# Attention's subtraction of q's maximum on GpSimd, and routing in five groups that cross the pairs

## The chip, the cores and the metric

The kernel runs on one core of a Trainium2 chip. The metric is the device time of one execution in microseconds, the median of several runs. The core has four compute engines that run side by side, each working through its own instructions in the order in which they were issued: TensorE (PE; its weight loads are shown as PEld), VectorE (DVE), ScalarE (ACT) and GpSimd (POOL). SyncE (SP), ACT and POOL issue DMA transfers. In the trace, SPq, ACTq, POOLq stand for what those engines' sequencers do.

## The reference

Three layers follow one another, all in float32. First linear attention over 8 batches and 8 heads of 576 tokens with 64 dimensions, then a mixture of 8 experts of which each token uses one, then a dense layer with a leaky activation:

```python
q_s = exp(q - max(q, -1));  q_s /= sum(q_s, -1) + 1e-9        # per token and head
k_s = exp(k - max(k, tokens));  k_s /= sum(k_s, tokens) + 1e-9
x = q_s @ (k_s^T @ v)                                          # [4608, 512]
logits = x @ w_gate + modality_bias[modality_id];  e = argmax(logits)
out[token] = prob(e) * (relu(x @ w1[e]) @ w2[e])
h = out @ w_in;  y = maximum(0.01 * h, h) @ w_out
```

## The kernel before

Attention with its routing is the first stage, up to about 193 us of the span; the experts, the hidden layer and the last product follow. Only the first stage is touched.

Batches are taken in four pairs. A pair is nine chunks of 128 tokens, so there are 36 chunks, counted through here from 0 to 35. For each pair `phase_k` works on k: `kmax` (DVE: a maximum over the tokens, L140, and two subtractions, L143), `kexp` (PE transposes, ACT exponentials), `kv` (PE products with v, L164), `krec` and `kvn` (normalise), `kvT` and `kg` (the gate's weights are multiplied in). `phase_q` takes the maximum of q over each head, for three chunks at once (`qmax`, L218), and subtracts it in place (`qsub`, L222), both on DVE. `phase_x` works chunk by chunk: `trans` transposes q on PE and exponentiates on ACT, `xmm` multiplies by k's result on PE and copies the denominators and the gate's logits to the tiles `ri` and `lr` on ACT, and `evac` takes the reciprocal of `ri` (L258) and scales the result out of PSUM (L260) on DVE, from where SP stores it to `xd`.

`phase_r` routes a group of chunks: some twenty small DVE instructions (`r0`, L296, to `r16`, L360), one exponential on ACT (`rx`) and two tiny PE products (`rm`) give each token a row in the table `region`. Then `scat` writes token and gate weight to that row by one indirect DMA for each chunk, issued from GpSimd (L363). `paced` puts a copy of one element of a chunk's `ri` ahead of a scatter on GpSimd (L375), so that the scatter waits until that chunk's reciprocal has been taken.

The order of all this is written out by hand. Every step has a key in chunk lengths (a pair starts at nine times its number; `evac` of chunk c has the key c + 1), the steps are sorted by key, and each engine gets its instructions in that order. The keys order the work; nothing waits for a clock. PSUM holds two chunks' results (`ps_x`), two transposed tiles (`ps_t`) and two of k's (`ps_k`).

Before, pair 0 is routed in one group with its nine scatters paced one chunk apart; pairs 1 to 3 in groups of three chunks, each group's scatters issued together 3.5 chunk lengths after its last chunk; ten groups in all. Behind the last scatter, the experts' first table entry is read from `region` (L546), the tokens' rows are gathered (L553), transposed (L564) and multiplied (L572). Meanwhile DVE works out the slot tables (L431 to L476). In the later hidden layer GpSimd adds tiles of 512 elements (L841, L842, L845) while DVE applies the leak (L814, both inputs in SBUF) and adds out of PSUM (L847).

Of the kernel before, what the change touches and what calls it, by code (L numbers as in the profile page):

```python
# [9 lines left out]
F32 = mybir.dt.float32  # L10
# [3 lines left out]
AF = mybir.ActivationFunctionType  # L14
ALU = mybir.AluOpType
# [4 lines left out]
B, H, S, D = 8, 8, 576, 64  # L20
NT, DM = B * S, H * D
NE, F1, F2 = 8, 1024, 2048
NPAIR = B // 2
NC = 9
# [67 lines left out]
def bc(ap, axis, n):  # L92
    a = ap.unsqueeze(axis)
    shape = list(a.shape)
    shape[axis] = n
    return a.broadcast_to(shape)


def attention(ctx, tc, cst, a, region, xd):

    nc = tc.nc
    ident, onesf, trib, onesb, biasT, tokid = cst["id"], cst["one"], cst["trib"], cst["oneb"], cst["biasT"], cst["tok"]
    kp = ctx.enter_context(tc.tile_pool(name="kp", bufs=2))
    sp = ctx.enter_context(tc.tile_pool(name="sp", bufs=2))
    one = ctx.enter_context(tc.tile_pool(name="one", bufs=1))
# [4 lines left out]
    eps = one.tile([128, 1], F32, name="eps")  # L110
    nc.vector.memset(eps, 1e-9)
    kvx = []
    for i in range(4):
        t = one.tile([128, 4, 146], F32, name=f"kvx{i}")
# [2 lines left out]
        nc.gpsimd.memset(t[64:128, :, 145:146], 1.0)  # L117
        kvx.append(t)
    tacc = cst["tacc"]
    kt, vt, qt, st_b = {}, {}, {}, {}  # L120

    def load_kv(i, hp):
        if hp == 0:
# [86 lines left out]
    def phase_q(i):  # L210
        s = {}

        def heads(n):
            return qt[i].rearrange("p c (h d) -> p (c h) d", d=D)[:, 24 * n:24 * n + 24]

        def qmax(n):
            qm = s[n] = sp.tile([128, 24], F32, tag="qm", name="qm")
            nc.vector.tensor_reduce(out=qm, in_=heads(n), axis=AX.X, op=ALU.max)  # L218

        def qsub(n):  # L220
            v = heads(n)
            nc.vector.tensor_tensor(out=v, in0=v, in1=bc(s[n][:, :], 2, D), op=ALU.subtract)  # L222

        tm, ts = ((0.2, 3.2, 9.5), (1.2, 4.2, 11.5)) if i == 0 else ((4.6, 7.5, 11.5), (5.5, 9.5, 13.5))
        return [(t, qmax, n) for n, t in enumerate(tm)] + [(t, qsub, n) for n, t in enumerate(ts)]

    def phase_x(i):
        s = {}

        def trans(c):  # L230
            tp = ps_t.tile([128, 4, 128], F32, tag="t", name="tq")
            for hp in range(4):
                nc.tensor.transpose(out=tp[:, hp], in_=qt[i][:, c, 128 * hp:128 * hp + 128], identity=ident)
            eq = s["eq", c] = sp.tile([128, 4, 128], F32, tag="eq", name="eq", bufs=3)
            nc.scalar.activation(out=eq, in_=tp, func=AF.Exp)

        def xmm(c):
            if c == 0:
                st_b[i] = (sp.tile([128, NC, 4, 16], F32, tag="lr", name="lr"), sp.tile([128, NC, 4, 2], F32, tag="ri", name="ri"))
            lr, ri = st_b[i]  # L240
            eq = s["eq", c]
            xp = s["xp", c] = ps_x.tile([128, 4, 256], F32, tag="x", name="xp")
            if c < 8:
                kx = kvx[(2 * i + c // 4) % 4]
                for hp in range(4):
                    nc.tensor.matmul(xp[:, hp, 0:146], lhsT=eq[:, hp], rhs=kx[:, hp], start=True, stop=True)
            else:
                for j in range(2):
                    kx = kvx[(2 * i + j) % 4]
                    for hp in range(4):  # L250
                        nc.tensor.matmul(xp[64 * j:64 * j + 64, hp, 0:146], lhsT=eq[:, hp, 64 * j:64 * j + 64],
                                         rhs=kx[:, hp], start=True, stop=True)
            nc.scalar.activation(out=ri[:, c], in_=xp[:, :, 144:146], func=AF.Identity, bias=eps[:, 0:1])
            nc.scalar.copy(out=lr[:, c], in_=xp[:, :, 128:144])

        def evac(c):
            ri = st_b[i][1]
            nc.vector.reciprocal(out=ri[:, c], in_=ri[:, c])  # L258
            xr = sp.tile([128, DM], F32, tag="xr", name="xr", bufs=4)
            nc.vector.tensor_tensor(out=xr.rearrange("p (q j d) -> p q j d", q=4, j=2),  # L260
                                    in0=s["xp", c][:, :, 0:128].rearrange("p q (j d) -> p q j d", j=2),
                                    in1=bc(ri[:, c], 3, D), op=ALU.mult)
            if c < 8:
                r0 = (2 * i + c // 4) * S + 128 * (c % 4)
                nc.sync.dma_start(out=xd[r0:r0 + 128], in_=xr)
            else:
                for j in range(2):
                    r0 = (2 * i + j) * S + 512
                    nc.sync.dma_start(out=xd[r0:r0 + 64], in_=xr[64 * j:64 * j + 64])

        l = []
        for c in range(NC):
            l += [(c - 0.9, trans, c), (c + 0.3, xmm, c), (c + 1.0, evac, c)]
        return l

    def phase_r(i, c0, c1):

        n = c1 - c0
        cs = slice(c0, c1)
        t, rp = {}, {}  # L280

        def r0():
            lr, ri = st_b[i]
            t["lp"] = sp.tile([128, NC, 8, NE], F32, tag="lp", name="lp", bufs=1)[:, 0:n]
            for x in ("lg", "ex", "w"):
                t[x] = sp.tile([128, NC, NE], F32, tag=x, name=x)[:, 0:n]
            for x in ("mx", "gs"):
                t[x] = sp.tile([128, NC], F32, tag=x, name=x)[:, 0:n]
            for x in ("oh", "st"):
                t[x + "f"] = sp.tile([128, 80], F32, tag=x, name=x)[:, 0:NE * (n + 1)]  # L290
                t[x] = t[x + "f"].rearrange("p (e c) -> p e c", e=NE)
            t["tot"] = sp.tile([128, NE], F32, tag="tot", name="tot")
            t["tb"] = sp.tile([128, 2, NE], BF16, tag="tb", name="tb")
            t["ix"] = sp.tile([128, NC], I32, tag="ix", name="ix", bufs=3)
            t["tg"] = sp.tile([128, NC, 2], F32, tag="tg", name="tg", bufs=3)
            nc.vector.tensor_tensor(out=t["lp"].rearrange("p c (q j) e -> p (c q) j e", q=4),  # L296
                                    in0=lr[:, cs].rearrange("p c q (j e) -> p (c q) j e", j=2),
                                    in1=bc(ri[:, cs].rearrange("p c q j -> p (c q) j"), 3, NE), op=ALU.mult)
            nc.scalar.copy(out=t["tg"][:, 0:n, 0], in_=tokid[:, NC * i + c0:NC * i + c1])

        def r1():
            nc.vector.tensor_reduce(out=t["lg"], in_=t["lp"].rearrange("p c h e -> p c e h"), axis=AX.X, op=ALU.add)

        def r2():
            nc.vector.tensor_tensor(out=t["lg"], in0=t["lg"], in1=biasT[:, NC * i + c0:NC * i + c1], op=ALU.add)

        def r3():
            nc.vector.tensor_reduce(out=t["mx"], in_=t["lg"], axis=AX.X, op=ALU.max)
# [62 lines left out]

    pace = one.tile([1, 1], F32, name="pace")

    def paced(i, c, scat, n):
        nc.gpsimd.tensor_copy(out=pace, in_=st_b[i][1][0:1, c, 0, 0:1])  # L375
        scat(n)

    steps = []
# [1 line left out]
    def add(t0, l):  # L380
        for x in l:
            steps.append((t0 + x[0], len(steps)) + tuple(x[1:]))

    for i in range(NPAIR):
        add(NC * (i - 1), phase_k(i) + phase_q(i))
        add(NC * i, phase_x(i))
        if i < 2:
            t0 = -100 + 10 * i
            add(t0, [(t, load_kv, i, hp) for hp, t in enumerate((0, 1, 3, 4))] + [(t, load_q, i, n) for n, t in enumerate((2, 5, 6))])
        else:  # L390
            t0 = NC * (i - 2)
            add(t0, [(0.5 * hp, load_kv, i, hp) for hp in range(4)] + [(7.9, load_q, i, n) for n in range(3)])

    def route(t0, i, c0, c1, times, ts):

        fs, scats = phase_r(i, c0, c1)
        t = 0
        for n, (name, f) in enumerate(fs.items()):
            t = times.get(name, t)
            add(t0 + t, [(0.001 * n, f)])  # L400
        for n, (f, c) in enumerate(scats):
            if isinstance(ts, tuple):
                add(t0 + ts[0] + n, [(0.0, paced, i + 1 + int(ts[0] + n - 1) // NC, int(ts[0] + n - 1) % NC, f, c)])
            else:
                add(t0 + ts, [(0.001 * n, f, c)])

    for i in range(1):
        route(NC * (i + 1), i, 0, NC, dict(r0=1.15, r1=2.5, r2=3.5, rx=4.4, r5=4.5, r8=5.6, rm=6.55, r10=6.6, r12=7.6, r13=7.61, r16=8.5), (9.05,))
    group = dict(r0=0.2, r2=0.6, rx=1.45, r5=1.15, rm=2.25, r10=2.1, r12=2.6)
    for i in range(1, NPAIR):  # L410
        for g in range(3):
            if (i, g) < (NPAIR - 1, 2):
                route(NC * i + 3 * g + 3, i, 3 * g, 3 * g + 3, group, 3.5)
    route(NC * NPAIR, NPAIR - 1, 6, NC, dict(r0=0.2), 0.5)
    add(1.0, [(0.1, cst["prep"])])
    for x in sorted(steps, key=lambda x: x[:2]):
        x[2](*x[3:])
# [573 lines left out]
def build(ctx: ExitStack, tc, a, out, dbg=None):  # L991
# [13 lines left out]
    with tc.manual_schedule():  # L1005
# [37 lines left out]
        with actx:  # L1043
            z = actx.enter_context(tc.tile_pool(name="zp", bufs=1)).tile([128, (NE * NT + SLOT) // 64], F32, name="z")
            nc.vector.memset(z, 0.0)
            nc.scalar.dma_start(out=region.rearrange("(p r) c -> p (r c)", p=128), in_=z)
            attention(actx, tc, cst, a, region, xd)
# [66 lines left out]
```

## Time and profile before

| | |
|---|---|
| median of 3 runs | 1421.89 us (1420.99 to 1422.07) |
| the profiled execution, its own time | 1421.04 us |
| its span in the trace | 1419.2 us |
| busy over the span | PE 1311.5 us (92%), DVE 1047.6 (74%), ACT 586.8 (41%), POOL 289.0 (20%) |
| mean granted TensorE clock | 0.972 of full speed |

The busy shares are means over all stages; the first stage, one seventh of the span, is read by itself below. In the trace's rows an engine's busy time counts instructions only, not the time in which its sequencer waits; the bracket at the end of a row is the engine's idle time before it and what ended that time.

### The profile page before, as it was taken

What the parts mean: (1) busy time and instruction counts of PE and PEld (TensorE: products, weight loads), DVE (VectorE), ACT (ScalarE), POOL (GpSimd) and SP (SyncE); (2) the same over time, 40 slices, a digit from 0 to 9 for tenths busy, and PEclk for the clock granted to TensorE, in tenths of its full rate; (3) what the DMA queues carried; (4) which work ended last, traced back from release to release, by engine and by line L of the source; (5) the groups of instructions that cost most, each with busy time, mean ns of one, the idle gap of its engine ahead of it and who ended that gap; (6) DMA issues with size and microseconds to landing.
All of it is one profiled execution on the core that took longest, in us unless ns stands there. A gap on an engine that the chain in (4) does not pass through costs nothing.

```text
span 1419.2 us, 23583 instructions
## 1 busy us (share of the span) xinstructions
PE 1311.5 (92%) x9189; PEld 1224.6 (86%) x9189; DVE 1047.6 (74%) x1504; ACT 586.8 (41%) x924; POOL 289.0 (20%) x249
## 2 busy tenths in 40 slices
PE   5987719999999999998999999999989999999998
PEld 5876717778777877787999999999989999999998
DVE  4889846867786777746677777787767777877785
ACT  3545415455545554556223323232333333333342
POOL 0004431101110011001334343434321101111111
PEclk9999869999999999999999999999999999999999
DMA  9763246778777878686933332333595343434330
GB/s 371 284 246 127 76 156 232 259 240 279 259 255 247 275 254 263 194 311 195 407 146 134 135 119 104 136 148 120 233 417 205 122 134 123 149 120 134 119 119 30
DMA packets 146970, 279.57 MB, mean 197 GB/s; under 512 B 18208, under 2 KB 70432, under 8 KB 145952
## 3 DMA queue, kind: packets, MB, share of 16 engines
q1 hardware_dynamic: 122064, 208.46, 43.1%
q10 hardware_dynamic: 17232, 48.48, 8.7%
q0 software_dynamic: 7552, 21.02, 4.1%
q8 instruction: 75, 1.23, 0.4%
q14 instruction: 47, 0.39, 0.1%
HBM read 181.59 MB, written 96.32 MB: 196 GB/s over the span
## 4 chain that ended last, share of the span: by engine, by line
issue 26%; DVE 8%; PE 7%; POOL 6%; DMA 3%; ACT 1%; POOLq 0%; SPq 0%; DVEq 0%
PE hp L801 7%; POOL out L982 3%; DMA wi<-wid 2%; POOL s L841 2%; DVE ht L814 1%; DMA hd<-ht 1%; DVE ht L850 1%; DVE ht L847 1%; DVE s L838 1%; DVE x L482 1%; DVE ht L834 1%; DVE s L836 1%; POOL s L842 1%; DVE xl L482 0%; ACT ht L843 0%
## 5 line engine op out<-in xcount | busy, mean ns | idle before, releaser
L801 PE MATMUL hp<-xh,wi 128*128 128x256 f32 x1152 | 212.8, 281 | 4.2 <-DVE ht L850 2.3
L960 PE MATMUL yp<-wi,x 128*128 128x256 f32 x1152 | 191.2, 283 | 0.6 <-DVE x L482 0.6
L801 PEld LDWEIGHTS hp<-xh,wi 128*128 128x128 f32 x1152 | 179.4, 188 | 6.8 <-DVE ht L850 3.7
L960 PE MATMUL yp<-wi,wi 128*128 128x256 f32 x1200 | 178.2, 283 | 0.3 <-DVE wi L482 0.3
L801 PE MATMUL hp<-x,wi 128*128 128x256 f32 x1296 | 164.5, 286 | 9.2 <-ACTq L708 6.4
L801 PEld LDWEIGHTS hp<-x,wi 128*128 128x128 f32 x1296 | 161.0, 195 | 9.6 <-ACTq L708 6.6
L960 PEld LDWEIGHTS yp<-wi,wi 128*128 128x128 f32 x1200 | 163.5, 192 | 0.5 <-DVE wi L482 0.5
L960 PEld LDWEIGHTS yp<-wi,x 128*128 128x128 f32 x1152 | 161.5, 192 | 0.8 <-DVE x L482 0.8
L801 PE MATMUL hp<-xl,wi 128*128 128x256 f32 x576 | 160.7, 279 | 0.0
L553 POOL DMA_INDIRECT xg<-xd,idi x44 | 55.6, 1264 | 398.6 <-DVE hl L575 331.6
L572 PE MATMUL hp<-xh,w1h 128*128 128x512 f32 (+1 forms) x320 | 122.9, 384 | 11.8 <-DVE hl L575 11.2
L583 PE MATMUL yp<-hh,w2h 128*128 128x512 f32 (+1 forms) x320 | 122.9, 384 | 0.0
L572 PE MATMUL hp<-xl,w1h 128*128 128x512 f32 (+1 forms) x320 | 121.6, 380 | 0.0
L572 PE MATMUL hp<-xh,w1l 128*128 128x512 f32 (+1 forms) x320 | 121.6, 380 | 0.0
L583 PE MATMUL yp<-hl,w2h 128*128 128x512 f32 (+1 forms) x320 | 121.5, 380 | 0.0
L583 PE MATMUL yp<-hh,w2l 128*128 128x512 f32 (+1 forms) x320 | 121.4, 379 | 0.0
L982 POOL DMA_INDIRECT out<-yo,idx x36 | 47.4, 1317 | 315.9 <-DVE idx L976 294.3
L482 DVE TENSOR_TENSOR w1l<-st,w1h 128x1024 fp32r<-128x1024 f32 x44 | 53.8, 1227 | 76.5 <-ACT w1h L481 74.1
L801 PEld LDWEIGHTS hp<-xl,wi 128*128 128x128 f32 x576 | 108.0, 187 | 0.0
L814 DVE SCALAR_TENSOR_TENSOR ht<-ht 128x1024 f32<-128x1024 f32 x72 | 104.9, 1457 | 2.5
L841 POOL TENSOR_TENSOR s<-s,s 128x512 f32<-128x512 f32 x36 | 48.7, 1352 | 209.3 <-DVE s L838 163.8
L843 ACT ACTIVATE ht<-s 128x512 f32<-128x512 f32 x36 | 22.8, 633 | 151.5 <-POOL s L842 147.0
(202 smaller groups left out, 2583.5 us busy)
## 6 DMA issues: line engine op xcount, KB each, us to landing
st<-in_w SPq DMA_DIRECT2D x89, 512.0 KB, 6.5
hd<-ht ACTq DMA_DIRECT2D x72, 512.0 KB, 2.9
xt<-hd SPq DMA_DIRECT2D x18, 1024.0 KB, 5.3
hr<-hd SPq DMA_DIRECT2D x18, 1024.0 KB, 5.2
wi<-wid SPq DMA_DIRECT2D x28, 512.0 KB, 10.3
wi<-wod SPq DMA_DIRECT2D x6, 2048.0 KB, 13.1
v<-in_v SPq DMA_DIRECT2D x16, 650.0 KB, 9.7
k<-in_k SPq DMA_DIRECT2D x16, 576.0 KB, 9.4
```

The lines of the kernel that those rows point to most:

```text
L482: nc.vector.tensor_tensor(out=lo, in0=src, in1=hi.bitcast(F32), op=ALU.subtract)
L553: nc.gpsimd.indirect_dma_start(out=xg[:, t], out_offset=None, in_=xd, in_offset=bass.IndirectOffsetOnAxis(ap=idi[:, t:t + 1], axis=0), bou ...
L572: nc.tensor.matmul(hp[:, rows], lhsT=w[:, k, 128 * f:128 * f + 128], rhs=x[:, k, rows], start=(n == 0), stop=(n == 11))
L583: nc.tensor.matmul(yp[:, rows], lhsT=w[:, f, 128 * d:128 * d + 128], rhs=h[:, f, rows], start=(n == 0), stop=(n == 23))
L801: self.nc.tensor.matmul(bank[:, g], lhsT=w[:, h, k, 128 * g:128 * g + 128], rhs=x[:, k], start=(n == 0), stop=(n == 5))
L814: V.scalar_tensor_tensor(out=c, in0=c, scalar=0.01, in1=c, op0=ALU.mult, op1=ALU.max)
L834: V.tensor_tensor(out=h[:, 0, 0], in0=bank, in1=s[1], op=ALU.add)
L836: V.tensor_tensor(out=s[6], in0=bank, in1=s[1], op=ALU.add)
L841: G.tensor_tensor(out=s[6], in0=s[6], in1=s[5], op=ALU.add)
L843: nc.scalar.activation(out=h[:, 1, 1], in_=s[5], func=AF.Relu)
L960: nc.tensor.matmul(bank, lhsT=x[:, k], rhs=w[i][:, h, k], start=(c == 0), stop=(c == 23))
L982: ins = nc.gpsimd.indirect_dma_start(out=out, out_offset=bass.IndirectOffsetOnAxis(ap=idi[s % 2][:, t:t + 1], axis=0), in_=y[:, t], in_off ...
```

## The change

`qsub` is issued on GpSimd instead of DVE, with the same operands, and the keys of `qmax` and `qsub` are moved, some by up to 1.5 chunk lengths earlier. `lr` and `ri` become one tile each for all 36 chunks. Routing works on any run of chunks: 0 to 8, 9 to 17, 18 to 26, 27 to 32 and 33 to 35, five groups, the third of them with a time table of its own (`mid`). The scatters of the first three groups are paced, 1.0, 0.7 and 0.5 chunk lengths apart; those of the fourth (six) and fifth (three) stand at the end, at the same key.

```diff
@@ phase_q
-            nc.vector.tensor_tensor(out=v, in0=v, in1=bc(s[n][:, :], 2, D), op=ALU.subtract)
-        tm, ts = ((0.2, 3.2, 9.5), (1.2, 4.2, 11.5)) if i == 0 else ((4.6, 7.5, 11.5), (5.5, 9.5, 13.5))
+            nc.gpsimd.tensor_tensor(out=v, in0=v, in1=bc(s[n][:, :], 2, D), op=ALU.subtract)
+        tm, ts = ((0.2, 3.2, 9.5), (1.2, 4.2, 10.5)) if i == 0 else ((4.6, 7.5, 11.0), (5.2, 8.5, 12.0))
@@ attention, phase_x, phase_r: one lr and one ri, indexed by NC * i + c
+    lr = one.tile([128, NPAIR * NC, 4, 16], F32, name="lr")
+    ri = one.tile([128, NPAIR * NC, 4, 2], F32, name="ri")
@@ pacing and routing
-    def paced(i, c, scat, n):
-        nc.gpsimd.tensor_copy(out=pace, in_=st_b[i][1][0:1, c, 0, 0:1])
+    def paced(c, scat, n):
+        nc.gpsimd.tensor_copy(out=pace, in_=ri[0:1, c, 0, 0:1])
         scat(n)
-            if isinstance(ts, tuple):
-                add(t0 + ts[0] + n, [(0.0, paced, i + 1 + int(ts[0] + n - 1) // NC, int(ts[0] + n - 1) % NC, f, c)])
+            if rate:
+                at = c1 + ts + rate * n
+                add(at, [(0.0, paced, min(int(at) - 1, NPAIR * NC - 1), f, c)])
             else:
-                add(t0 + ts, [(0.001 * n, f, c)])
+                add(c1 + ts, [(0.001 * n, f, c)])
-    for i in range(1):
-        route(NC * (i + 1), i, 0, NC, dict(r0=1.15, r1=2.5, r2=3.5, rx=4.4, r5=4.5, r8=5.6, rm=6.55, r10=6.6, r12=7.6, r13=7.61, r16=8.5), (9.05,))
-    group = dict(r0=0.2, r2=0.6, rx=1.45, r5=1.15, rm=2.25, r10=2.1, r12=2.6)
-    for i in range(1, NPAIR):
-        for g in range(3):
-            if (i, g) < (NPAIR - 1, 2):
-                route(NC * i + 3 * g + 3, i, 3 * g, 3 * g + 3, group, 3.5)
-    route(NC * NPAIR, NPAIR - 1, 6, NC, dict(r0=0.2), 0.5)
+    slow = dict(r0=1.15, r1=2.5, r2=3.5, rx=4.4, r5=4.5, r8=5.6, rm=6.55, r10=6.6, r12=7.6, r13=7.61, r16=8.5)
+    mid = dict(r0=0.2, r1=0.9, r2=1.2, rx=2.1, r5=2.15, r8=2.6, rm=3.3, r10=3.4, r12=4.1, r16=4.6)
+    fast = dict(r0=0.2, r2=0.6, rx=1.45, r5=1.15, rm=2.25, r10=2.1, r12=2.6)
+    route(0, 9, slow, 9.05, 1.0)
+    route(9, 18, slow, 9.05, 0.7)
+    route(18, 27, mid, 5.05, 0.5)
+    route(27, 33, fast, 3.5)
+    route(33, 36, dict(r0=0.2), 0.5)
```

## Rows read from the trace of the kernel before

**Rows 1.** Windows: busy us of each engine (instructions), granted clock, DMA share, GB/s.
```profile
45.50:77.70 32.20, 30.02 (x258) 28.80 (x257) 27.19 (x49) 19.84 (x62) 0.00 (x0) 1.00 0.72 262
77.70:120.30 42.60, 34.37 (x272) 32.58 (x271) 39.44 (x109) 21.42 (x72) 6.24 (x6) 0.92 0.58 218
120.30:151.20 30.90, 23.75 (x188) 22.45 (x186) 26.94 (x80) 15.49 (x51) 16.80 (x23) 0.89 0.17 61
151.20:192.60 41.40, 19.97 (x144) 18.11 (x141) 34.80 (x143) 10.84 (x41) 17.64 (x17) 0.82 0.22 71
```
After the window and its length the order is PE, PEld, DVE, ACT, POOL.

**Rows 2.** Timeline of DVE: start, us, engine, line, operation [idle before].
```profile
145.75 0.16 DVE L170 TENSOR_SCALAR rk<-kvp 128x2 f32<-128x2 f32 x1 [0.47 <-PE kvp L164]
...
147.48 0.20 DVE L258 RECIPROCAL ri<-ri 128x8 f32<-128x8 f32 x1 [0.87 <-ACT ri L253]
```

**Rows 3.** Timeline around one subtraction on DVE.
```profile
167.88 1.75 DVE L222 TENSOR_TENSOR q<-q,qm 128x1536 f32<-128x1536 f32 x1
169.55 0.20 DVE L258 RECIPROCAL ri<-ri 128x8 f32<-128x8 f32 x1
169.70 0.72 PEld L233 LDWEIGHTS tq<-cf,q 128*128 128x128 f32 x4 [4.07 <-issue]
```

**Rows 4.** Timeline from the last scatters to the experts' first matmul.
```profile
185.91 1.02 POOL L363 DMA_INDIRECT region<-tg,ix  x1 [3.93 <-issue]
...
191.65 0.99 POOL L363 DMA_INDIRECT region<-tg,ix  x1 [0.30 <-issue]
...
194.00 0.36 SPq L546 DMA_DIRECT2D idt<-region  x1
...
212.99 0.78 PE L572 MATMUL hp<-xh,w1h 128*128 128x512 f32 x1
```

**Rows 5.** DVE by line and shape, 0 to 200 us: busy us, mean ns, idle before.
```profile
L222 DVE TENSOR_TENSOR q<-q,qm 128x1536 f32<-128x1536 f32 x12 | 20.9, 1745 | 0.0
...
L302 DVE TENSOR_REDUCE lg<-lp 128x24 f32<-128x192 f32 x9 | 4.5, 503 | 0.3
L296 DVE TENSOR_TENSOR lp<-lr,ri 128x192 f32<-128x192 f32 x9 | 3.2, 353 | 0.0
...
L302 DVE TENSOR_REDUCE lg<-lp 128x72 f32<-128x576 f32 x1 | 1.2, 1198 | 0.0
...
L296 DVE TENSOR_TENSOR lp<-lr,ri 128x576 f32<-128x576 f32 x1 | 0.8, 751 | 0.0
```

**Rows 6.** Timeline of DVE, first and last of the last group's 20 instructions.
```profile
181.16 0.35 DVE L296 TENSOR_TENSOR lp<-lr,ri 128x192 f32<-128x192 f32 x1
...
184.97 0.17 DVE L360 CAST ix<-mx 128x3 int32<-128x3 f32 x1
```

**Rows 7.** Timeline of DVE and POOL in the hidden layer.
```profile
683.04 1.29 POOL L845 TENSOR_TENSOR ht<-ht,s 128x512 f32<-128x512 f32 x1 [1.41 <-ACT s L844]
683.35 1.53 DVE L814 SCALAR_TENSOR_TENSOR ht<-ht 128x512 f32<-128x512 f32 x1
...
804.99 0.69 DVE L814 SCALAR_TENSOR_TENSOR ht<-ht 128x512 f32<-128x512 f32 x1
...
809.14 0.69 DVE L847 TENSOR_TENSOR ht<-hp,s 128x512 f32<-128x512 f32 x1 [1.47 <-POOL s L841]
809.19 1.30 POOL L842 TENSOR_TENSOR s<-s,s 128x512 f32<-128x512 f32 x1
```

**Rows 8.** POOL by line and shape, 0 to 200 us.
```profile
L115 POOL MEMSET kvx<- 128x584 f32 x4 | 2.4, 588 | 0.5 <-POOLq L1106 0.3
```

**Rows 9.** Timeline of POOL: scatters and paced scatters of the first group.
```profile
148.44 0.97 POOL L363 DMA_INDIRECT region<-tg,ix  x1 [0.30 <-issue]
...
149.73 0.98 POOL L363 DMA_INDIRECT region<-tg,ix  x1 [0.16 <-issue]
...
151.52 0.18 POOL L375 COPY pace<-ri 1x1 f32<-1x1 f32 x1 [0.80 <-DVE ri L258]
152.26 0.98 POOL L363 DMA_INDIRECT region<-tg,ix  x1 [0.57 <-issue]
```

## What I predict, before seeing the result

> **What bounds the kernel now.** I read the page's forty slices first, to see which stretch holds everything the change touches: attention with its routing, up to about 193 us of the span. Then I cut that stretch with the windows view at the reciprocals of chunks 0, 9, 18 and 25 and at the end of the last scatter [rows 1], because the order written out by hand is in chunk numbers. The reader should compare DVE with PE in each row. In the first window (chunks 0 to 9) PE is busy 30.0 of 32.2 us at full clock, DVE only 27.2. In the second DVE is busy 39.4 of 42.6, PE 34.4 at a mean clock of 0.92; counted by instructions (272 against 258 in the first row) PE would need 31.7. In the third DVE is busy 26.9 of 30.9; what is left is mostly two waits for a chunk, 0.5 and 0.9 us [rows 2], and some reading latency. In the fourth DVE is busy 34.8 of 41.4, and the rest is the tail, in which GpSimd issues scatters.
>
> The timeline says the same in small: the DVE subtraction at 167.88 takes 1.75 us, and the transposes of the chunks that it feeds begin at 169.70, when it ends [rows 3]. So pair 0 is bound by PE, pairs 1 and 2 by DVE, pair 3 by DVE and then by the scatters. What comes after cannot start early: the last scatter goes out at 191.65, the expert phase reads the table at 194.00, and its first matmul stands at 212.99 [rows 4]. This chain only moves with the last scatter, so a microsecond won or lost there is one at the end.
>
> **What leaves DVE.** Twelve subtractions at 1.745 us [rows 5]; 1.66 us from start to start, as one overlaps its neighbour a little. Two lie before 45 us, where the loads set the pace and nothing is gained. Of the other ten, three fall in window 1, three in window 2, two in window 3, two in window 4.
> Routing: ten groups become five. A group of three chunks takes 20 DVE instructions, 3.9 us from 181.16 to the end at 185.14 [rows 6]. For nine chunks the reduction grows from 503 to 1198 ns and the product from 353 to 751 [rows 5], so I take 5.0 us, and 4.5 for six. By the keys, window 2 loses groups 9:12 and 12:15 and a third of 15:18 (9.1 us), window 3 exchanges 8.7 us of small groups for most of 9:18 (4.9): 3.8; window 4 exchanges 17.3 for 13.5: 3.8.
> DVE left to do: window 2, 42.6 - 5.0 - 9.1 = 28.5; window 3, 30.9 - 1.3 (the two waits) - 3.3 - 3.8 = 22.5; window 4 up to the last group's end, 33.9 (151.2 to 185.14) - 3.3 - 3.8 = 26.8.
>
> **What GpSimd takes on.** It shows no 1536-element subtraction. Its nearest row is a 128x512 add at 1.29 us [rows 7], three times which is 3.9; from below, its memset of 584 elements at 588 ns [rows 8] would give 1.55. The row of the same operation is nearest: 3.7. From a maximum to the first transpose that needs it the written order leaves at least 3.1 chunk-lengths (for chunks 15, 24 and 33), about 9 us, so a subtraction that starts at once is in time. Four of them stand in GpSimd's queue behind copies that wait for a chunk's reciprocal, and PE's transposes wait behind them in turn; the closest is pair 3's third, behind five scatters: by the sum below it ends some 18.5 us after chunk 25's reciprocal, and chunk 33 is due at about 20. The maxima stay on DVE, half a chunk earlier in places; the single `lr` and `ri` tiles and the new order issue no load or store that was not there.
>
> **What it costs DVE.** The two engines are not independent. DVE's two-input operation on 512 elements takes 0.69 us at 804.99, with no add beside it. At 683.35, begun 0.3 us into a GpSimd add, it takes 1.53 and ends 0.55 us after that add; an operation with one input in PSUM, at 809.14, takes 0.69 beside an add [rows 7]. So a DVE instruction with both inputs in SBUF waits until GpSimd's instruction is over, and an evacuation does not. With the subtraction running for 3.7 us after its maximum, I ask what DVE meets next in the written order. In window 2: third subtraction of pair 1, two evacuations and two reductions, nothing within 3.7 us. First of pair 2: `tacc`'s sum after 1.35 us, so 2.35 lost. Second of pair 2: the scan after 0.3, so 3.4 lost. In window 4: second of pair 3, the product of group 18:27, 3.4 lost; third of pair 3, inside the same group's chain, about 2. In the other places it first meets a subtraction of k's maximum or another one-input operation. No row has one of these beside a GpSimd add: nothing by the evacuation's row, the full rest (1.2 in window 3 at the k subtraction, 2.7 at the denominator) by the two-input row; I take the middle, 1.95 in window 3, and keep both ends.
> The Trainium skill, "SBUF — State Buffer", section "Who interferes with whom", calls this an exclusive lock held for the whole instruction and counts a one-input DVE copy or scalar operation in a two-port mode among those that block. The trace agrees for two inputs (1.53 against 0.69 us) and shows nothing for one; by that rule window 3 would lose 3.9 instead of 1.95.
>
> Window 2 is then 28.5 + 5.75 = 34.25, beside PE's 31.7; window 1 shows that two nearly equal engines lose some time to each other (32.2 for 30.0), so I add 1.5: 35.7, a gain of 6.9. Window 3: 22.5 + 1.95 + 0.6 = 25.0, a gain of 5.9. Window 1 is PE's: a gain of 0.7 at most of the 2.2 that PE does not use. Sum of the gains: 13.5.
>
> **What the scatters cost.** All 36 remain, at 1.0 us each, but they bunch later. From chunk 25 on GpSimd now has, in this order: the ninth scatter of group 0:9, a subtraction, five scatters, a subtraction, thirteen scatters, then nine more (six of 27:33 and three of 33:36, interleaved); before, the window held 16 scatters and no subtraction. A paced scatter that waits costs 2.05 us from the reciprocal (copy 0.18, gap, transfer ended at 153.24); one that is not kept waiting follows at 1.29 (148.44 to 149.73, its copy inside) [rows 9]. I take 1.35 for those eighteen, 1.3 for the last nine (185.91 to 191.65 is 1.43 each, with DVE's table work beside them [rows 4]), 3.85 for a subtraction with its gap, and 1.1 for the wait for chunk 28: 2.05 + 7.7 + 24.3 + 11.7 + 1.1 = 46.9 us. From below 44.6 (1.29 each throughout, no wait), from above 52.4 (1.72 for each paced one, 151.52 to 153.24, a copy that never hides). DVE's own path is 26.8 + 5.4 of waiting + 0.8 (185.14 to 185.91) + 8 scatters behind the last group's first (10.4) = 43.4, shorter: here GpSimd becomes the bound. Before, the stretch took 41.4. Loss: 5.5. The table work on DVE, 7 us behind the last group, is over before the scatters and stays hidden.
>
> Sum: 0.7 + 6.9 + 5.9 - 5.5 = 8.0 us. The profiled execution took 1421.04 us (span 1419.2), so 1413.0; the median of the runs is 0.85 above it: 1413.9, say 1414.
>
> **The rivals.** Differences under 0.2%, 2.8 us, are about what a measurement cannot tell from none.
> *The engines hardly meet* (0.14): what falls beside a subtraction has one input. Then window 2 is PE's at 32.5, window 3 23.0, and the scatters go at their lower bound: 0.7 + 10.1 + 7.9 - 3.2 = 15.5, so 1406.4. For it: only two clear collisions in window 2. Against: the pair of 0.69 and 1.53.
> *One-input operations are held as well* (0.14): window 3 takes 27.0 and gains 3.9, so 1416. In window 1 PE covers the two holds of 1.3 us. That is the rule of the page named above; the trace has no row for or against it.
> *The gain is given back by GpSimd's queue* (0.12): each paced scatter costs its full 1.72, the last window takes 52.4, loses 11.0, and 2.5 us are left: 1419.4, no change that can be told. For it: the waiting copies [rows 9]; against: those that hide.
> *DVE is held for the whole of each subtraction* (0.18): ten holds of 3.7 in place of ten instructions of 1.66. Window 1 becomes 34.8 (2.6 lost), window 2 41.1 (1.5 won), window 3 30.6 (0.3 won), and the last loses 6.5 as its group 18:27 comes late: 7.3 slower, 1429. It decides from a mean hold of about 3 us; I count 1.4. For it: DVE, once stopped, stops the evacuations, and so PE, behind it.
> That nothing changes at all is excluded by the rows: DVE is what the second window waits for, and the order of the scatters differs.
>
> **Numbers.** My forecast has 0.42, its own range 1409 to 1419. Faster: 0.42 + 0.14 + 0.10 of the held one-input case = 0.66; no change 0.12 + 0.04 = 0.16; slower 0.18. The range for 8 in 10 reaches from the first rival to within the last: 1406 to 1425.
>
> **What would show it.** The subtraction as a GpSimd row of 3.4 to 3.9 us; DVE instructions stretched beside it (the scan and `tacc`'s sum above all) and the evacuations not; the stretch from chunk 9's reciprocal to chunk 18's at 34 to 37 us; GpSimd issuing without a pause from chunk 28 to the read of the table; the last scatter some 47 us after chunk 25's reciprocal and near 184 us of the span. Wrong if the subtraction takes over 5 us, if a transpose waits for it, or if the scatters keep up so well that DVE's last group still sets the end.

## The result and the profile after

The changed kernel takes 1409.27 us (median; 1407.18 to 1410.61), the kernel before 1421.44 beside it on the same chip: a ratio of 0.9914, 95% interval 0.9897 to 0.9931, so 12.2 us faster. I had said 1414, in a range of 1406 to 1425. The profiled execution took 1407.18 us, with a span of 1405.4. The helpers have moved by a line or two: the subtraction is L224, an evacuation L259.

First the same four windows as in [rows 1], cut at the reciprocals of the same chunks (start, length, then PE, PEld, DVE, ACT, POOL, granted clock, DMA share, GB/s):

```profile
45.90:76.60 30.70, 29.89 (x258) 28.87 (x257) 22.92 (x47) 19.75 (x62) 8.28 (x3) 1.00 0.75 263
76.60:110.80 34.20, 30.63 (x260) 28.88 (x259) 31.07 (x61) 20.02 (x64) 9.48 (x5) 1.00 0.71 267
110.80:135.20 24.40, 23.31 (x199) 22.03 (x198) 22.19 (x49) 16.10 (x53) 13.72 (x17) 1.00 0.27 88
135.20:180.30 45.10, 19.22 (x133) 16.66 (x132) 35.52 (x114) 10.27 (x37) 37.17 (x49) 0.76 0.22 65
```

The windows gained 1.5, 8.4 and 6.5 us and the last one lost 3.7. PE and DVE are now about level in the second window (30.6 and 31.1 of 34.2), PE is the busier engine of the third, and the granted clock is at the upper level throughout the first three (before: 0.92 and 0.89 in the second and third). In the fourth, POOL is the busiest engine, where it was DVE.

Then GpSimd's timeline, its subtractions from the first of the pair of chunks 18 to 26 on (start, us, operation, idle before):

```profile
92.30 2.76 POOL L224 TENSOR_TENSOR q<-q,qm 128x1536 f32<-128x1536 f32 x1 [7.22 <-DMA xd<-xr]
...
101.88 2.76 POOL L224 TENSOR_TENSOR q<-q,qm 128x1536 f32<-128x1536 f32 x1 [6.81 <-DVE oh L345]
118.87 2.77 POOL L224 TENSOR_TENSOR q<-q,qm 128x1536 f32<-128x1536 f32 x1
128.79 2.77 POOL L224 TENSOR_TENSOR q<-q,qm 128x1536 f32<-128x1536 f32 x1
...
137.28 2.77 POOL L224 TENSOR_TENSOR q<-q,qm 128x1536 f32<-128x1536 f32 x1
...
148.57 2.77 POOL L224 TENSOR_TENSOR q<-q,qm 128x1536 f32<-128x1536 f32 x1
```

(92.30 and 101.88 are the first and second of that pair's three, 118.87 its third; the other three belong to the last pair.) And DVE's timeline, the instructions that fell beside them:

```profile
93.22 1.87 DVE L327 CAST tb<-tacc 128x8 bf16<-128x8 f32 x1
...
101.91 2.91 DVE L349 TENSOR_TENSOR_SCAN st<-cf,oh 128x80 f32<-128x80 f32 x1
...
129.64 1.96 DVE L342 TENSOR_SCALAR gs<-gs 128x9 f32<-128x9 f32 x1
...
137.27 3.40 DVE L294 TENSOR_TENSOR lp<-lr,ri 128x576 f32<-128x576 f32 x1
...
148.67 2.70 DVE L342 TENSOR_SCALAR gs<-gs 128x9 f32<-128x9 f32 x1
```

With no subtraction beside them the same operations take 0.16, 0.33, 0.17, 0.75 and 0.17 us. The reader should lay the two lists over each other: each long DVE instruction ends within 0.7 us of the end of a GpSimd subtraction (148.57 + 2.77 = 151.34; 148.67 + 2.70 = 151.37). I call the time that such an instruction takes beyond its usual one a hold. Three of the five have one input only. An evacuation, a reduction and a reciprocal that begin inside a subtraction are not held; the row that I had read for the evacuation before (809.14 in [rows 7]) began 0.05 us ahead of the GpSimd addition and could not show it, these can:

```profile
82.32 2.76 POOL L224 TENSOR_TENSOR q<-q,qm 128x1536 f32<-128x1536 f32 x1 [12.28 <-DVE qm L220]
82.55 0.69 DVE L259 TENSOR_TENSOR xr<-xp,ri 128x512 f32<-128x512 f32 x1 [0.20 <-DVE ri L257]
...
83.42 1.19 DVE L300 TENSOR_REDUCE lg<-lp 128x72 f32<-128x576 f32 x1
84.54 0.19 DVE L257 RECIPROCAL ri<-ri 128x8 f32<-128x8 f32 x1
...
L259 DVE TENSOR_TENSOR xr<-xp,ri 128x512 f32<-128x512 f32 x36 | 24.9, 692 | 7.7 <-DVE ri L257 2.4 <-ACT ek L162 1.7 <-PE rp L333 0.4
```

The last is a row of the groups by shape (busy us, mean ns, idle before): 692 ns on average over all 36 evacuations. Last, the timeline at the end of the stage, to compare with [rows 4]:

```profile
168.67 0.17 DVE L358 CAST ix<-mx 128x3 int32<-128x3 f32 x1
...
168.86 0.97 POOL L361 DMA_INDIRECT region<-tg,ix  x1 [0.30 <-issue]
...
179.31 0.97 POOL L361 DMA_INDIRECT region<-tg,ix  x1 [0.30 <-issue]
...
181.64 0.37 SPq L546 DMA_DIRECT2D idt<-region  x1
...
200.64 0.78 PE L572 MATMUL hp<-xh,w1h 128*128 128x512 f32 x1
```

DVE is done with its last group at 168.84; nine scatters are still to go out, one every 1.3 us, and the table is read at 181.64 instead of 194.00. The first expert matmul comes 12.35 us earlier, about the 12.2 of the medians.

### The profile page after: what moved, and what is told of

It reads as the page before. It is cut to its first block, busy times and chain, and to the rows that moved or that the text cites. A ratio compares the mean times of both kernels' runs of the same rounds, so it can differ in the third digit from the quotient of the medians.

```text
span 1405.4 us, 23487 instructions
## 1 busy us (share of the span) xinstructions
PE 1306.8 (93%) x9179; PEld 1219.4 (87%) x9179; DVE 1029.1 (73%) x1392; ACT 585.5 (42%) x914; POOL 322.0 (23%) x279
## 4 chain that ended last, share of the span: by engine, by line
issue 26%; DVE 8%; PE 8%; POOL 6%; DMA 3%; ACT 1%; POOLq 0%; SPq 0%; DVEq 0%; ACTq 0%
PE hp L801 8%; POOL out L982 3%; POOL s L841 2%; DMA wi<-wid 2%; DMA hd<-ht 2%; DVE ht L814 1%; DVE ht L847 1%; DVE ht L850 1%; DVE s L838 1%; DVE x L482 1%; DVE ht L834 1%; DVE s L836 1%; POOL s L842 1%; DVE xl L482 0%; ACT ht L843 0%
## 5 line engine op out<-in xcount | busy, mean ns | idle before, releaser
L801 PE MATMUL hp<-x,wi 128*128 128x256 f32 x1296 | 164.2, 286 | 8.0 <-DVEq L708 6.5
L801 PEld LDWEIGHTS hp<-x,wi 128*128 128x128 f32 x1296 | 160.7, 194 | 8.3 <-ACTq L708 6.6
L801 PE MATMUL hp<-xl,wi 128*128 128x256 f32 x576 | 160.7, 279 | 0.0
L572 PE MATMUL hp<-xh,w1h 128*128 128x512 f32 (+1 forms) x320 | 122.9, 384 | 12.7 <-DVE hl L575 11.6
```

What stands on the lines that cost most here:

```text
L572: nc.tensor.matmul(hp[:, rows], lhsT=w[:, k, 128 * f:128 * f + 128], rhs=x[:, k, rows], start=(n == 0), stop=(n == 11))
L801: self.nc.tensor.matmul(bank[:, g], lhsT=w[:, h, k, 128 * g:128 * g + 128], rhs=x[:, k], start=(n == 0), stop=(n == 5))
```

## The experiments

All ratios are against the kernel before; the changed kernel stands at 0.9914. The experiments are numbered in the order in which they ran and told in the order of the argument. Windows are cut as above.

**Experiment 1: the subtractions back on DVE, the merged groups kept.**

```diff
-            nc.gpsimd.tensor_tensor(out=v, in0=v, in1=bc(s[n][:, :], 2, D), op=ALU.subtract)
+            nc.vector.tensor_tensor(out=v, in0=v, in1=bc(s[n][:, :], 2, D), op=ALU.subtract)
```

> The changed kernel with the twelve subtractions back on DVE and everything else (keys, five groups, pacing) as changed. My theory: merging the routing groups paid nearly everything, and the move to GpSimd nearly nothing, because each subtraction that leaves DVE (1.66 us) comes back as holds (1.7 and 2.6 us in the second window, 1.8 in the third). So: window 1 +0.8, window 2 +0.7, window 3 +1.5, last window -2.3 (GpSimd's chain is 5.5 us shorter, then DVE's last group and the eight scatters behind it set the end): about 0.7 us slower than the changed kernel, 1410 (1408 to 1413). Rival, the move is what pays: ten times 1.66 us come back, 1420 or more. Rival, GpSimd's chain alone sets the whole result: 5.5 us faster, 1404.

1415.43 us, 0.9957 (0.9943 to 0.9972): a miss. The merging (with the new keys, the pacing and the single `lr` and `ri` tiles kept, which no run takes apart) is worth 6 us without the move, and the move is worth another 6 on top of it, more than I had left for it. The second window takes 35.9 us (34.2 in the changed kernel), the third 25.6 (24.4), the last 47.8 (45.1). The first takes 32.2 us, as in the kernel before, and 30.7 in experiment 2, which has the move without the merging: the 1.5 us of that window are the move's. The last number is not the subtractions' alone: in this profile ACT stands still near its end (below).

**Experiment 2: the move alone, the ten old groups kept.** The kernel before with `nc.gpsimd` in `qsub` and the new keys of `qmax` and `qsub`.

> The kernel before with the subtractions on GpSimd at their new keys, and the old ten groups and scatters. My theory: the subtractions leave DVE (16.6 us over ten) but DVE is held beside most of them by one-input and two-input operations alike, about 2 us each; window 2 and 3 together win 2 to 4 us, the tail has no bunched scatters, so nothing is lost there: 1418 (1414 to 1421). Rival, the move is what pays: 1410 or less. Rival, holds cost more than the move brings: 1422 or more.

1422.3 us, 1.0003 (0.9992 to 1.0014): a miss too, no change at all, as the rival had it by which holds cost more than the move brings. So 6 from the one part, 0 from the other, 12 from both: the parts don't add up. The trace says why. DVE by line and shape, 76 to 185 us:

```profile
L351 DVE TENSOR_TENSOR_SCAN st<-cf,oh 128x32 f32<-128x32 f32 x8 | 10.4, 1299 | 0.0
...
L344 DVE TENSOR_SCALAR gs<-gs 128x3 f32<-128x3 f32 x8 | 4.6, 569 | 0.3
...
L351 DVE TENSOR_TENSOR_SCAN st<-cf,oh 128x80 f32<-128x80 f32 x1 | 2.9, 2906 | 0.0
```

The scan of a group of three takes 215 ns in the kernel before, 1299 on average here. The timelines of DVE and POOL show single ones:

```profile
128.49 2.89 DVE L351 TENSOR_TENSOR_SCAN st<-cf,oh 128x32 f32<-128x32 f32 x1
128.51 2.77 POOL L222 TENSOR_TENSOR q<-q,qm 128x1536 f32<-128x1536 f32 x1
...
142.51 3.00 DVE L351 TENSOR_TENSOR_SCAN st<-cf,oh 128x32 f32<-128x32 f32 x1
142.66 2.77 POOL L222 TENSOR_TENSOR q<-q,qm 128x1536 f32<-128x1536 f32 x1
```

Six instructions are held in this stretch: four scans (2.9, 2.9, 3.0 and 3.5 us) and two additions to the denominator (1.8 and 1.7). Less what they take anyway (0.33, 0.21 and 0.17), that is 14.5 us, against seven subtractions of 1.66 that left DVE there, 11.6 us. The gain is used up by the holds.

**Experiment 9: the move alone, at other places in DVE's order.** If that is so, the same work at other places must pay. Experiment 2 with, for pairs 1 to 3, each maximum and subtraction put behind the scan of the group before:

```diff
-        ... else ((4.6, 7.5, 11.0), (5.2, 8.5, 12.0))
+        ... else ((5.65, 8.65, 11.65), (5.66, 8.66, 11.66))
```

> The kernel before with the subtractions on GpSimd and its ten groups kept, as in the second experiment, but each maximum and subtraction of q for pairs 1 to 3 stands behind the scan of the group before it (5.65, 8.65, 11.65 chunks instead of 4.6, 7.5, 11.0). If the move alone paid nothing because DVE was held for 2.9, 2.9, 3.0 and 3.5 us at scans that came up while GpSimd subtracted, then no scan takes over 1 us, the holds fall from some 13 us to under 5, and the time is 1414 us (1411 to 1417). The rival: what the move alone lacks is the merging of the groups, wherever the subtractions stand, and the time stays at 1420 to 1424.

1415.38 us, 0.9956 (0.9943 to 0.9969): as expected. The same view as in experiment 2:

```profile
L296 DVE TENSOR_TENSOR lp<-lr,ri 128x192 f32<-128x192 f32 x9 | 10.7, 1192 | 0.0
L351 DVE TENSOR_TENSOR_SCAN st<-cf,oh 128x32 f32<-128x32 f32 x9 | 1.9, 207 | 0.0
L344 DVE TENSOR_SCALAR gs<-gs 128x3 f32<-128x3 f32 x9 | 1.6, 176 | 0.3
```

The scan is back at 207 ns and the addition at 176. What is held now is the product that begins the next group (four of nine, 2.1 to 2.5 us; 1192 ns on average instead of 353), 7.6 us of holds where experiment 2 had 14.5, and three subtractions of k's maximum are held 0.3 to 0.4 us each; that is more than the 5 I had allowed. The time fell by 6.9 us. The second window falls from 43.9 to 40.5 us, the third from 33.7 to 26.8, together more than the 6 to 7 us of holds that are gone; the granted clock rose with them (0.96 and 0.94 for 0.88 and 0.85). Not an instruction was taken out and only places were changed, so what the move is worth hangs on where it stands in DVE's order.

**Experiment 10: no subtraction on any engine.** The changed kernel without the line that issues `qsub` (q is not shifted before the exponential; the maxima are formed).

> The changed kernel without its twelve subtractions on any engine (the maxima are still formed; the shift of q before the exponential is left out). What the subtractions still cost there is then all gone: holds of some 10 us on DVE in the stretch from chunk 9 on, a wait of 1.5 us of TensorE, and 2.8 us of GpSimd's queue each. If they are what my sum said, the stretches from chunk 9 to 18, 18 to 25 and 25 to the last scatter become 32, 23.5 and 40 us, and the time is 1400 us (1397 to 1403). The rival: TensorE bounds the stretches anyway and the scatters the last one, and the time is 1405 to 1409.

1399.32 us, 0.9856 (0.9839 to 0.9873): as expected, with windows of

```profile
76.30:108.84 32.54, 30.55 (x260) 28.95 (x259) 26.80 (x61) 20.08 (x64) 1.31 (x2) 1.00 0.76 284
108.84:131.12 22.28, 21.98 (x190) 21.12 (x188) 20.46 (x49) 15.55 (x50) 8.09 (x14) 1.00 0.24 84
131.12:171.19 40.07, 18.88 (x141) 16.93 (x139) 29.81 (x114) 10.58 (x39) 31.25 (x47) 0.79 0.24 74
```

So twelve subtractions cost some 9 us on GpSimd (the last scatter ends at 171.19 instead of 180.28; the medians are 10 apart, the ratios 8) and 16 on DVE (experiment 1, its standstill of ACT included). Five of the 9 are in the last window, where they stand in GpSimd's queue.

**Experiment 4: smaller holds.** Each subtraction as three of 512 elements.

```diff
-            nc.gpsimd.tensor_tensor(out=v, in0=v, in1=bc(s[n][:, :], 2, D), op=ALU.subtract)
+            for g in range(3):
+                w = slice(8 * g, 8 * g + 8)
+                nc.gpsimd.tensor_tensor(out=v[:, w], in0=v[:, w], in1=bc(s[n][:, w], 2, D), op=ALU.subtract)
```

> The changed kernel with each subtraction cut into three GpSimd instructions of 512 elements. My theory: a hold lasts to the end of the one instruction that is running, so holds fall from 1.7 to 2.7 us to under 1.0 each; window 2 falls from 34.2 to about 32 (PE, busy 30.6 of it, is then the bound), window 3 by 0.5 at most, the last window does not fall, since GpSimd's chain is there the bound and gets some 0.3 us longer for each subtraction: 1407 (1405.5 to 1408.5). Rival, DVE waits until GpSimd's queue is idle: the holds stay as long, 1409 to 1410.

1413.01 us, 0.9941 (0.9929 to 0.9953): a miss. The mechanism works where I looked for it: the scan that took 2.91 us takes 1.19, so DVE waits for the GpSimd instruction under way and gets in before the next, and the second window falls to 33.4 us. But the product behind that scan, at 100.11, is then held by the next third, 0.89 us instead of 0.23: the two holds together are 1.5 us, not 0.86. The last window takes 50.9, 5.8 longer. ACT's timeline there:

```profile
166.82 0.27 ACT L254 ACTIVATE ri<-xp,eps 128x8 f32<-128x8 f32 x1 [8.81 <-remote]
```

It waits for PE's product for chunk 35 and nothing else in the program; that product ended at 159.64 (157.87 and 1.77), 7.2 us before.

**Experiments 3, 5, 6, 11 and 7: GpSimd's queue in the last window.** In experiment 3 the six scatters of chunks 27 to 32 go ahead of the last three:

```diff
-    route(27, 33, fast, 3.5)
+    route(27, 33, fast, 3.4)
```

> The changed kernel with the six scatters of group 27:33 ahead of the last group's three instead of interleaved with them (one key, 3.4 for 3.5). My theory: GpSimd's queue is what ends last, and it has the same nine scatters to issue behind the paced ones, so nothing changes: 1409 within 1.5 us, the last scatter again 45 us after chunk 25's reciprocal. Rival, DVE's last group sets the end (its first scatter waits for DVE and eight follow): now three follow, 5 to 6 us less, 1404.

1410.04 us, 0.9918 (0.9904 to 0.9931): the same, as expected, though in its profile ACT stands still (below) and the last window takes 47.6 us, not 45. In experiment 5 the second group is routed early, with the third's keys:

```diff
-    route(9, 18, slow, 9.05, 0.7)
+    route(9, 18, mid, 5.05, 0.5)
```

> The changed kernel with group 9:18 on the time table of group 18:27 (its scatters start 5.05 chunk lengths after its last chunk, half a chunk apart, instead of 9.05 and 0.7). Nine of the 27 scatters behind chunk 25 then lie before it, and GpSimd's last stretch loses some 12 us of its 45.1. My theory: two chains end together there. DVE's is 33.7 us from chunk 25's reciprocal to the last group's end, 0.8 to its first scatter, and eight scatters of 1.28 behind the same queue: 44.7. So the end moves by half a microsecond only: 1409 (1407 to 1411). Rival, GpSimd's chain alone is the bound: 4 to 8 us less, 1401 to 1405.

1413.06 us, 0.9945 (0.993 to 0.996): a miss. Experiment 6 has both edits:

> The same, and the six scatters of group 27:33 ahead of the last three, which changed nothing by itself. My theory: GpSimd has time for the six while DVE works on the last group, so only three follow it: 33.7 + 0.8 + 3.8 = 38.3; the slot tables on DVE, 7 us behind the last group and 1.9 to the read of the table, then end last, the read comes at 42.5 after chunk 25's reciprocal instead of 46.5: 4 us less than the changed kernel, 1405 (1403 to 1407). Rival, the chain ahead of DVE's last group has grown or ACT stands still there for some other reason: 1408 or more.

1410.73 us, 0.9925 (0.9909 to 0.9942): a miss. PE's timeline of experiment 5 names a wait that the changed kernel has in small (1.50 us, at 151.39):

```profile
149.54 1.12 PE L235 MATMUL tq<-cf,q 128*128 128x128 f32 x4 [6.03 <-POOL q L224]
```

The maximum ended at 136.95 and its subtraction began at 146.71, behind paced scatters in GpSimd's queue; the transposes waited for it. Experiment 11 is experiment 6 with the last pair's second and third subtraction on DVE:

> The changed kernel with the second group of chunks routed early and the fourth group's scatters ahead of the last three, as in the sixth experiment, and the second and third subtraction of pair 3 back on DVE, as in the eighth. If the early group lost because its scatters stood in GpSimd's queue ahead of those subtractions (TensorE waited 6.0 us for one in the fifth), that wait is gone, DVE's last group ends near 168, three scatters behind it at 172, the table work at 176, and the time is 1402 us (1400 to 1404). The rival: the early group costs DVE its place in the stretch from chunk 18 to 25 (27.2 instead of 24.4 us), and the time is 1406 to 1410.

1408.43 us, 0.9919 (0.9904 to 0.9934): a miss. The wait is gone, but the rival has it: the second and third windows take 35.1 and 27.1 us (34.3 and 24.4 in experiment 8, below), so the early group takes 3.5 us from the stretch in which DVE and PE have none to spare. Experiment 7 is the changed kernel with unpaced scatters, no copies ahead of them.

> The changed kernel without the copies that make a scatter wait for a reciprocal; the order is kept. My theory: in the last stretch GpSimd's third subtraction of pair 3 still waits for its maximum, so GpSimd's chain gets about 4 us shorter (3.4 of waits ahead of that subtraction, 0.05 for each copy behind it), and DVE's chain of 44.7 us then ends last: half to one microsecond less, 1408.5 (1407 to 1410). Rival, the pacing itself keeps something else fast (loads, DVE) and its loss costs: 1411 or more. Rival, the pacing copies are what the tail loses: 1405.

1409.84 us, 0.9917 (0.99 to 0.9934): the pacing copies cost nothing that can be measured, as expected. But in its trace two effects cancel: the third window takes 26.9 us instead of 24.4 and the last 43.3 instead of 45.1.

```profile
135.75 2.76 POOL L224 TENSOR_TENSOR q<-q,qm 128x1536 f32<-128x1536 f32 x1 [0.88 <-DVE oh L345]
135.77 2.92 DVE L349 TENSOR_TENSOR_SCAN st<-cf,oh 128x80 f32<-128x80 f32 x1
...
172.07 0.98 POOL L361 DMA_INDIRECT region<-tg,ix  x1 [2.51 <-issue]
```

Without the copies a subtraction comes earlier and meets the scan in the third window (2.92 us; 0.33 in the changed kernel), and in the last GpSimd stands idle for 2.51 us and goes on 0.77 us after DVE's last group has ended (171.30): with GpSimd's queue shortened, DVE's path sets the end.

**Experiment 8: fewer subtractions in GpSimd's queue.** The last pair's second and third subtraction back on DVE, the other ten on GpSimd.

```diff
+            eng = nc.vector if i == NPAIR - 1 and n else nc.gpsimd
+            eng.tensor_tensor(out=v, in0=v, in1=bc(s[n][:, :], 2, D), op=ALU.subtract)
```

> The changed kernel with only pair 3's second and third subtraction back on DVE. My theory: the last stretch loses the two holds (2.65 and 2.5 us) and gains two subtractions of 1.66 on DVE, so DVE's chain is 42.8, and GpSimd's is 39.6 for 45.1: 2.3 us less than the changed kernel, 1407 (1405 to 1409). Rival, the subtractions pay on GpSimd everywhere: 1411 or more. If ACT stands still for some microseconds near chunk 33, as it did in the run with all twelve on DVE, the gain is lost: 1409 to 1411.

1405.62 us, 0.9884 (0.9865 to 0.9902): as expected, and the lowest median here of a kernel that computes everything, though its interval overlaps that of the changed kernel: that it is faster is not shown. The last window:

```profile
136.36:179.08 42.72, 18.20 (x133) 15.98 (x132) 33.46 (x116) 10.20 (x37) 34.56 (x47) 0.81 0.22 69
```

45.1 us have become 42.7; as the first window began 1.2 us later in this profile, the last scatter ends only 1.2 us earlier, at 179.08. DVE takes two subtractions of 1.75 us, is rid of two holds of 2.65 and 2.5, and GpSimd gets 5.5 us of its queue back.

**Experiment 12: the remaining holds moved.** Experiment 8 with the keys of two maxima and two subtractions shifted so that no held instruction of its trace falls beside one.

```diff
+        if i == 2:
+            tm, ts = (5.65, 7.63, 11.0), (5.66, 8.5, 12.0)
+        if i == 3:
+            ts = 5.0, 8.5, 12.0
```

> The eighth experiment (the second and third subtraction of pair 3 on DVE) with the holds that its trace shows taken away by place alone: for the pair of chunks 18 to 26 the first maximum and subtraction stand behind the running sum instead of ahead of it, the second behind the scan instead of ahead of it, and for the last pair the first subtraction stands one scatter earlier in GpSimd's queue. There the conversion took 1.87 us, the scan 2.91 and the addition to the denominator 1.97, against 0.16, 0.33 and 0.17. If holds are what the subtractions on GpSimd still cost, none of the three takes over 0.7 us, the stretch from chunk 9 to 18 falls from 34.3 to 32.5 to 33.3 us, and the time is 1403 us (1401 to 1405). The rival: other instructions are held in their place, or TensorE bounds the stretch, and the time stays at 1405 to 1408.

1408.48 us, 0.9902 (0.9886 to 0.9919): a miss, and not below experiment 8. Its windows and one row each of DVE and ACT:

```profile
77.51:110.47 32.96, 30.52 (x260) 28.94 (x259) 27.55 (x61) 20.08 (x64) 9.60 (x5) 1.00 0.76 286
110.47:134.77 24.30, 22.71 (x193) 21.47 (x192) 22.12 (x48) 15.67 (x51) 13.61 (x16) 1.00 0.22 78
134.77:181.83 47.06, 20.08 (x139) 18.26 (x136) 33.52 (x116) 10.67 (x40) 34.98 (x47) 0.72 0.21 62
```

```profile
127.49 1.87 DVE L332 CAST tb<-tacc 128x8 bf16<-128x8 f32 x1
...
158.93 0.27 ACT L257 ACTIVATE ri<-xp,eps 128x8 f32<-128x8 f32 x1 [4.23 <-remote]
```

The step did its work in the second window, 32.96 us, 0.4 from the 32.54 without any subtraction. In the third another conversion was held in place of the addition to the denominator, and nothing was won. In the last window ACT stood still for 4.23 us, 2.8 of them after the product that it needs had ended (156.16), and the window is 4.3 us longer than experiment 8's.

## Why the prediction came out right, step by step

| stretch | predicted | measured |
|---|---|---|
| window 1 | gain 0.7 | 1.5 |
| window 2 | gain 6.9 (35.7 us) | 8.4 (34.2 us) |
| window 3 | gain 5.9 (25.0 us) | 6.5 (24.4 us) |
| window 4 | loss 5.5 (46.9 us) | 3.7 (45.1 us) |
| start of window 1 | as before | 0.4 later |
| last scatter ended | 184 | 180.28 |

Signs and order were right in all four; the total was short by 4.4 us (8.0 for 12.4, as the end of the last scatter moved from 192.64 to 180.28). The four errors all have one direction, and 1409.27 lies at the lower edge of the 1409 to 1419 that I had given the forecast itself. One of my own signs of being wrong came true in small: a transpose did wait for a subtraction (below).

**Window 1.** I allowed 0.7 of the 2.2 us that PE does not use; the move gained 1.5 there (experiments 1 and 2). PE's bound was right; how much of PE's idle time there came from DVE was put too low.

**The subtraction on GpSimd** is the term that was mis-sized: 3.7 us taken, 2.76 measured, within my bounds of 1.55 and 3.9 but below the row I called nearest. It enters twice. In the last window two of them stand in the queue, 1.9 us less, about that window's error (46.9 against 45.1). In the second window it makes the holds shorter.

**The holds** were placed rightly. Window 2: 2.35 at the `tacc` step and 3.4 at the scan, 5.75; measured 1.71 and 2.58, 4.3. At the `tacc` step it was not the sum with its two inputs that was held but the conversion just ahead of it, at 93.22, which has one. Window 4: 3.4 at the product and about 2 in the same group's chain; measured 2.65 and 2.5. The 1.45 us by which window 2 was less held are its error.

**One input.** In window 3 I took the middle between nothing and the full rest, 1.95, and the denominator's addition was held 1.8 us. The rest of 2.7 that I had for it was too long by 0.9, and the k subtraction was not met. That the middle came out is luck: one of the two was held in full and the other missed. And the 0.6 that I added in that window has no row behind it. One-input operations are held: a conversion of 8 elements took 1.87 instead of 0.16 us, an addition of a constant to 9 elements 2.70 instead of 0.17, and at 35.42, ahead of the windows, a subtraction of k's maximum 1.3 us longer than usual. The rule of the Trainium skill, "SBUF — State Buffer", section "Who interferes with whom", that one-input copies, conversions and scalar operations of DVE can be blocked too, is borne out by the trace. That an instruction waits for the one under way and no longer is what experiment 4 shows (a third of the length, 0.86 us of hold at the scan instead of 2.58). The rival by which one-input operations are held still gave 1416: it too had the subtraction at 3.7, and the k subtraction among the held.

**The groups.** Merging was given 9.1 us of DVE in window 2 and 3.8 in each of the two behind it; experiment 1, which has it without the move, shows 42.6 to 35.9 us in window 2 and 30.9 to 25.6 in window 3. In the second window this is most of the gain (6.7 of 8.4), as in my sum, in which 5.0 us of subtractions were paid for with 5.75 of holds.

**GpSimd as the bound of the last window** is right: from 147 us on it does not pause (the paced scatters at 154.27 and 155.59 are 1.32 apart, 1.35 taken), and DVE ends 11 us before the last scatter. But DVE's own path is hardly shorter: its last group, due 32.2 us after chunk 25's reciprocal by my sum, ended 33.7 us after it, at 168.84, and that group's first scatter began at 170.13, where 0.77 us lay between the two before (184.97 and 0.17, 185.91). I had DVE's path at 43.4 beside 46.9; the two end within about half a microsecond of each other.

What I had called "in time" was not quite: the last subtraction held PE's transposes up for 1.50 us.

```profile
151.39 0.83 PE L235 MATMUL tq<-cf,q 128*128 128x128 f32 x3 [1.50 <-POOL q L224]
```

That subtraction ended 16.2 us after chunk 25's reciprocal (18.5 by my sum), but PE was ready for chunk 33 after 14.7, not 20.

Of the rivals, DVE held for the whole of every subtraction (1429) needed a mean hold of 3 us over ten subtractions. Measured are 1.71, 2.58, 1.8, 2.65 and 2.5, two of 0.2 and 0.3 at subtractions of k's maximum in window 1, and none at the other three: 1.2 on average (I had counted 1.4). It was nearer than it looked: in experiment 2 the same move with other neighbours meets 14.5 us of holds in seven subtractions and gains nothing. I had read the collisions off one order and did not say how much hung on it.

What stays open: how the 6 us of the move on top of the merging divide between DVE's own time, holds, queue and ACT's standstill, since the standstill shows in the profile of experiment 1 and not in that of the changed kernel.

## What to carry to other kernels

Before elementwise work is moved from DVE to GpSimd, write down which DVE instruction stands next in its order: a product or a scan with two inputs in SBUF, a conversion or an operation with a constant, however small, waited until the GpSimd instruction was over, and the same move paid 0 or 6 us depending on its place alone. Prefer places where PSUM evacuations, reductions and reciprocals follow. Cutting the GpSimd instruction up shortened the holds where such a place wasn't there, but the kernel as a whole did not gain by it here. Near the end of a stage count GpSimd's queue as well as DVE's: two subtractions fewer there made the last window 2.4 us shorter in the profile, and the 3.5 us of work that DVE took back were less than the 5.2 us of holds that went; that the whole kernel gained by it is not clear of the noise.

## What the hardware showed that I had not expected

GpSimd's subtraction of 1536 elements, the second operand broadcast over 64, takes 2.76 us, 1.8 ns an element; its addition of two full operands of 512 takes 1.29, 2.5 ns [rows 7]. In three of 512 it takes 1043 ns each, 2.0 ns an element.

In the profiles of experiments 1, 3, 4 and 12, ACT stands still for 3.9 to 8.8 us near chunks 33 to 35, in front of an instruction whose only input had been written before, and the trace names no instruction of the program for it. The last window of experiment 4 is 5.8 us longer with it. In the changed kernel and in experiment 8, ACT idles at the same place for 4.5 and 5.1 us, but PE's product ends there too, so nothing would be seen. In all six traces an instruction queue has a transfer between 157 and 165 us, but only in experiment 1 does it fall into the standstill (164.2; ACT stood from 162.8 to 167.5). In experiments 3 and 4 it came before (161.1 and 157.1; ACT stood from 166.0 and 158.0 on), in experiment 12 behind (160.7; ACT went on at 158.9). That ACT waits for these transfers is not shown, and the cause stays open.
